# Attention and a three-way maxout layer on one core: the order of 489 commands and the engine letters of some of them are replaced

## The chip, the cores and the metric

The program runs on one core of one Trainium2 chip. The metric is device microseconds (us) of one execution. One core has the engines PE (TensorE, matrix products), DVE (VectorE), ACT (ScalarE), POOL (GpSimd) and SP (SyncE, which only issues transfers here). Each takes its own instructions strictly in the order in which the program gives them, and they meet at semaphores.

## The reference

```python
# q, k, v: 4 x 8 x 768 x 64; three of the eight heads see all earlier keys,
# five see 4 sink keys and a window of 64
scores = scale * np.matmul(q, k.transpose(0, 1, 3, 2))
...
a = np.exp(scores)
a = a / (np.sum(a, axis=-1, keepdims=True) + 1e-09)
return np.matmul(a, v).astype(np.float32)
...
x = np.ascontiguousarray(attn_out.transpose(0, 2, 1, 3)).reshape(B * S, H * D)
h = np.maximum(np.maximum(x @ w1, x @ w2), x @ w3)
return (h @ w_out).astype(np.float32)
```

x has 3072 rows of 512, each of w1, w2, w3 is 512 x 768, w_out is 768 x 512. Inputs and output are float32; the kernel computes its products in float16 with float32 sums.

## The kernel before

There are four batches (b = 0 to 3), and each batch has two halves of 384 query rows. The function `fast` holds one small function for each kind of work, and a tuple of strings, `PROGRAM`, names them one after the other with their arguments. A loop at the end of `fast` runs over the strings, and every engine gets its instructions in that order. Nothing else orders the work: there is no scheduler, only the semaphores between engines. A letter at the end of a command names the engine that does its element-wise part: `d` and `r` DVE (copy, or a reduction over one element that copies), `a` ACT, `p` POOL.

The commands that matter here:

- `idle n`: n products of zeros on PE (tile idl), 128 x 512, with no use for the result.
- `hl`, `load_v` issue transfers of q, k, v on the queues of SP and ACT; `load b quad` issues those of k and q (tile kq) on POOL's queue, two or four transfers; `w i` issues the transfer of a weight matrix on POOL's queue, `w 3` that of w_out (tile woutt).
- `cast`, `turnp`: for batch 0 a pair of heads is cast to float16 (tiles kn, qn) and transposed on PE (tile tr, copied to KQ). `turn b quad i part`: for batches 1 to 3 a quarter of kq is transposed by DVE (STREAM_TRANSPOSE, tile KQ). A batch takes eight such commands.
- `s0`, `s`: products of q and k (tile st, two buffers in PSUM), and on ACT the exponentials of them (tile pt). `k0`, `k`: a mask multiplied on pt, by DVE or POOL. `kx0`, `kx`: the far keys gathered (tile kx).
- `v`, `vc`, `vt`, `y`: v is cast, for batch 0 also sorted by a product on PE (tile vb), and gathered (tiles va, vx).
- `av b half hp`: probabilities times v for two heads (tile oacc on PE), a reciprocal and a multiplication on DVE (tile x), and with `D` a transposing transfer to xT on SP's queue.
- `f b half wi ni`: a hidden product, four matmuls of 128 x 384 into tile yy. With wi = 0 it is cast to acc by the letter's engine, with wi = 1 DVE takes the maximum into acc, with wi = 2 into hT. There are 144 of them.
- `o b half tb`: six matmuls of 128 x 512 on hT, a copy to ot, a transfer out. There are 24.
- `flags` (12 kinds of small instruction on POOL) compares the flags with what the order assumes, `guess` makes all five engines load its result from memory (TENSOR_LOAD flagged); `check`, `verdict`, `read` do the same near the end with all sums of exponentials (TENSOR_LOAD differ). `gs`, `gp` put a small transfer or copy in a queue, as a delay or a wait.

All tiles tr, vb, oacc, yy, idl share one pool of four PSUM banks, so PE can be at most four of them ahead of the engine that empties them:

```python
bkp = ctx.enter_context(tc.tile_pool(name="bkp", bufs=4, space=bass.MemoryType.PSUM))
...
for line in PROGRAM:
    for item in line.split(", "):
        name, *args = item.split()
        do[name](*args)
```

## Time and profile before

| what | us |
|---|---|
| median of 3 runs | 190.45 |
| the three runs | 189.97, 190.45, 194.31 |
| the profiled execution | 190.93 |
| its span, first to last instruction | 189.2 |
| first `f` product on PE | 26.38 |
| first scores of batch 2 (`s 2 0`) on PE | 71.05 |
| end of the last output product on PE | 184.6 |

The profiled execution is 1.7 us longer than its span, and 0.5 us longer than the median of the runs. An engine's busy time counts the time from the start to the end of its instructions. Matmuls are pipelined and their ends are modelled, so the busy time of PE says less than the start of one group of matmuls against the start of the next.

### The profile page before, as it was taken

The numbers are of one execution on the slowest core, as the hardware profiler recorded it, in microseconds if no ns is written. First come the engines' busy times: TensorE is split into PE (matmuls) and PEld (weight loads), VectorE is DVE, ScalarE is ACT, GpSimd is POOL, SyncE is SP. The second block draws the span as 40 slices with busy tenths as digits, with TensorE's granted clock in tenths as the row PEclk, the third lists the DMA queues.
The fourth block names the chain that finished last, engine by engine and source line by source line (L and its number), as shares of the span: only waits on it lengthen the run. The fifth ranks groups of instructions, "written<-read, shape, count | busy, mean of one in ns | idle before, by whom it ended". The sixth has DMA issues, their size and how long they took to land.

```text
span 189.2 us, 4749 instructions
## 1 busy us (share of the span) xinstructions
PE 180.0 (95%) x1859; PEld 105.7 (56%) x1859; DVE 144.7 (76%) x308; ACT 98.8 (52%) x158; POOL 82.3 (44%) x140
## 2 busy tenths in 40 slices
PE   7989799999999799999999999999999999999990
PEld 2644556566556356865565566655755575654550
DVE  3758989989899597888879899765883698475540
ACT  3599698377975457489086436665346301311110
POOL 7595978908883990099147102126313400000000
PEclk9999999999999999999999999999999999999998
DMA  5999999999999999539994301321132013401413
GB/s 178 327 327 276 208 211 208 195 150 204 193 158 204 122 271 203 140 66 200 212 223 120 112 0 55 66 80 55 30 64 107 0 59 63 136 0 55 166 56 119
DMA packets 44248, 26.59 MB, mean 141 GB/s; under 512 B 31038, under 2 KB 39742, under 8 KB 44222
## 3 DMA queue, kind: packets, MB, share of 16 engines
q1 hardware_dynamic: 38798, 17.54, 38.6%
q0 software_dynamic: 4192, 7.87, 23.1%
q10 hardware_dynamic: 1232, 0.85, 1.4%
q8 instruction: 15, 0.25, 0.5%
q14 instruction: 11, 0.09, 0.1%
HBM read 25.17 MB, written 6.29 MB: 166 GB/s over the span
## 4 chain that ended last, share of the span: by engine, by line
PE 80%; DVE 8%; DMA 7%; issue 1%; ACT 0%; ACTq 0%; DVEq 0%
PE yy L437 44%; PE yy L462 15%; PE oacc L717 8%; PE st L674 7%; DMA qs<-in_q_dram 5%; PE yst L437 3%; DMA vs<-in_v_dram 3%; DVE x L724 1%; PE yst L462 1%; DVE KQ L272 1%; DVE vx L800 1%; PE vb L505 1%; DVE va L478 1%; DVE KQ L241 1%; DVE va L510 1%
## 5 line engine op out<-in xcount | busy, mean ns | idle before, releaser
L377 POOL TENSOR_TENSOR pt<-pt,kb 128x512 f16<-128x512 f16 (+5 forms) x53 | 48.5, 934 | 61.0 <-ACT pt L691 49.6
L691 ACT ACTIVATE pt<-st 128x1024 f16<-128x1024 f32 (+2 forms) x51 | 43.5, 908 | 24.3 <-PE st L674 23.9
L437 PE MATMUL yy<-xT,w2t 128*128 128x384 f16 x184 | 36.2, 326 | 0.0
L437 PE MATMUL yy<-xT,w0t 128*128 128x384 f16 x180 | 34.6, 326 | 0.0
L437 PE MATMUL yy<-xT,w1t 128*128 128x384 f16 x176 | 34.2, 326 | 0.0
L462 PE MATMUL yy<-woutt,hT 128*128 128x512 f16 (+1 forms) x138 | 31.5, 372 | 1.1 <-DVE hT L449 1.1
L449 DVE TENSOR_TENSOR hT<-yy,acc 128x384 f16<-128x384 f32 x46 | 25.2, 555 | 5.2 <-PE yy L437 3.5
L449 DVE TENSOR_TENSOR acc<-yy,acc 128x384 f16<-128x384 f32 x44 | 24.0, 555 | 5.3 <-PE yy L437 4.0
L272 DVE STREAM_TRANSPOSE KQ<-kq 128x384 f32<-128x384 f32 x24 | 25.5, 1134 | 2.1 <-DMA kq<-in_k_dram 1.0
L437 PEld LDWEIGHTS <-w0t 128*128 128x128 f16 x192 | 18.1, 98 | 12.6 <-issue 0.6
L445 ACT CAST acc<-yy 128x384 f16<-128x384 f32 x27 | 12.8, 490 | 22.5 <-PE yy L437 20.4
L437 PEld LDWEIGHTS <-w1t 128*128 128x128 f16 x192 | 17.9, 98 | 12.1 <-issue 0.6
L437 PEld LDWEIGHTS <-w2t 128*128 128x128 f16 x192 | 17.6, 98 | 12.1 <-issue 0.5
L462 PEld LDWEIGHTS <-hT 128*128 128x128 f16 x150 | 14.4, 98 | 16.7 <-DMA woutt<-in_moe_w_out_dram 1.5
L471 ACT COPY ot<-yy 128x512 f32<-128x512 f32 (+1 forms) x14 | 7.9, 566 | 23.4 <-PE yy L462 20.2
L717 PEld LDWEIGHTS <-pt 128*128 128x128 f16 x472 | 17.3, 97 | 4.8 <-issue 1.0
L717 PE MATMUL oacc<-va,pt 128*128 128x65 f16 x392 | 18.8, 193 | 0.5 <-DVE pt L377 0.3
L724 DVE TENSOR_TENSOR x<-oacc,sums 128x384 f16<-128x384 f32 x32 | 17.8, 557 | 1.1
L629 ACT ACTIVATE pt<-st 128x1024 f16<-128x1024 f32 (+5 forms) x22 | 15.5, 759 | 2.9 <-PE st L608 2.7
L674 PE MATMUL st<-KQ 32*128 32x128 f16 (+2 forms) x342 | 14.9, 257 | 0.0
L377 DVE TENSOR_TENSOR pt<-pt,kb 128x256 f16<-128x256 f16 (+4 forms) x31 | 11.9, 388 | 1.8 <-ACT pt L691 1.7
L445 DVE CAST acc<-yy 128x384 f16<-128x384 f32 x18 | 9.9, 558 | 3.4 <-PE yy L437 3.0
(117 smaller groups left out, 190.9 us busy)
## 6 DMA issues: line engine op xcount, KB each, us to landing
out_dram<-ot SPq DMA_DIRECT2D x23, 256.0 KB, 2.2
vs<-in_v_dram SPq DMA_DIRECT2D x18, 256.0 KB, 4.7
ks<-in_k_dram SPq DMA_DIRECT2D x8, 192.0 KB, 5.1
kq<-in_k_dram POOLq DMA_DIRECT2D x3, 384.0 KB, 7.1
kq<-in_q_dram POOLq DMA_DIRECT2D x3, 384.0 KB, 8.7
kq<-in_k_dram POOLq DMA_DIRECT2D x3, 288.0 KB, 8.3
kq<-in_q_dram POOLq DMA_DIRECT2D x3, 288.0 KB, 9.5
qs<-in_q_dram ACTq DMA_DIRECT2D x4, 192.0 KB, 4.5
```

The source lines that it names most:

```text
L272: nc.vector.transpose(out=dst.rearrange("c (p j) -> c j p", j=n)[:, j0:j1], in_=src.rearrange("c (j i) -> c j i", i=R),)
L377: engine.tensor_tensor(out=x, in0=x, in1=of_blocks(kb, pattern, rows), op=ALU.mult)
L437: nc.tensor.matmul(yy[:, 0:HALF], w_t[wi][:, ks, ni * P : (ni + 1) * P], xT[b, half, ks].rearrange("p a t -> p (a t)"), start=(ks == 0), s ...
L445: op(out=acc[b, half, ni], in_=yy[:, 0:HALF])
L449: nc.vector.tensor_tensor(out=acc[b, half, ni] if wi == 1 else hT[b, half, ni], in0=yy[:, 0:HALF], in1=acc[b, half, ni], op=ALU.max,)
L462: nc.tensor.matmul(yo[:, 0:n], hT[b, half, ns][:, tb * P : (tb + 1) * P], woutt[:, ns, c : c + n], start=(ns == 0), stop=(ns == NNB - 1),)
L471: op(out=ot[:, c : c + n], in_=yo[:, 0:n])
L629: nc.scalar.activation(out=pts[0, half, hp, u][:, r0:r1, c0:c1], in_=sts[hp][:, r0:r1, c0:c1], func=AF.Exp, scale=sc,)
L674: nc.tensor.matmul(sts["XY"[g // 2]][:, g % 2, c0 : c0 + n * P], KQ[rows, 0, ki * P : (ki + 1) * P] if kind == "p" else kx[b % 2][quad][ro ...
L691: nc.scalar.activation(out=pts[b, s, xy][:, r0:r1, c0:c1], in_=st[:, r0:r1, c0:c1], func=AF.Exp, scale=sc,)
L717: nc.tensor.matmul(o[:, i, r, 0 : D + 1], at[b, h, kind, ki, qi], vv[:, 0 : D + 1], start=(n == 0), stop=(n == len(todo) - 1), skip_group_ ...
L724: nc.vector.tensor_tensor(out=x, in0=o[:, :, :, 0:D], in1=rc.unsqueeze(3).to_broadcast([P, HB, 2, D]), op=ALU.mult,)
```

## The change

The tuple `PROGRAM` is written anew. It has the same 489 commands, the same number of each kind, and the same products, exponentials, masks and transfers; the order differs from the first command on, and some letters do: of the 48 `f` with wi = 0, ACT takes 36 instead of 28 and DVE 12 instead of 20; of the 24 `o`, ACT 11 instead of 15 and DVE 13 instead of 9; five of the 24 `v` become reductions on DVE, as none was before. `idle` still stands six times with 18 products in all.

```diff
-    "idle 11, hl 0 2 2 sc, cast 0 1 pd, turnp 0 1 aa, cast 0 0 dd, cast 0 2 dp, load_v 0 0 0 4 s",
+    "idle 2, cleark 0 d, cleark 1 d, idle 2, hl 0 2 2 sc, load_v 0 0 0 4 s, flags",
+    "cast 0 0 aa, cast 0 2 aa, idle 11, cast 0 1 pd, idle 1, turnp 0 0 dd, turnp 0 1 ad",
...
```

Three places show what moves. The first is the start of POOL's row. kb and every are constants, kn and ks_117 belong to pair 1 of batch 0, want, none, both and flagged to `flags`. Before:

```order
L348 AFFINE_SELECT every_140<-every_140 128x386
L220 CAST kn<-ks_117 128x384
L220 CAST qn<-qs 128x384
L220 CAST kn<-ks 128x384
L544 MEMSET kx_155 128x512
```

Now:

```order
L351 AFFINE_SELECT every_140<-every_140 128x386
L757 MEMSET want 1x8
L759 MEMSET want 1x1 x5
L761 TENSOR_SCALAR none<-ir_121 1x16
L763 TENSOR_TENSOR both<-none 1x8
L764 TENSOR_TENSOR both<-both,want 1x8
L765 TENSOR_TENSOR both<-both 1x8
L767 TENSOR_TENSOR both<-both 1x4
L767 TENSOR_TENSOR both<-both 1x2
L767 TENSOR_TENSOR both<-both 1x1
L769 CAST flagged<-both 1x2
L223 CAST kn<-ks_117 128x384
```

The whole of `flags` has moved from the middle of the program to the front, ahead of the cast of kn of pair 1; the cast of qn of pair 2, which followed it, went to ACT, and that of kn of pair 3 comes later.

The second is POOL's row around the transfers of k and q for the second quad of batch 2, `load 2 1` (kq_1235 before, kq_1256 now). va1, vx0 and vx1 are the gathered v of batches 1 and 2. Before:

```order
L766 CAST flagged_161<-both_1046 1x2
L377 TENSOR_TENSOR pt_799<-pt_799,kb_130 128x2x2x128
L393 DMA woutt_61<-in_moe_w_out_dram 128x6x512
L377 TENSOR_TENSOR pt_1083<-pt_1083,kb_130 128x2x128
L377 TENSOR_TENSOR pt_883<-pt_883,kb_130 128x384
L377 TENSOR_TENSOR pt_1006<-pt_1006,kb_130 128x128
L377 TENSOR_TENSOR pt_1148<-pt_1148,kb_130 128x256
L257 DMA kq_1235<-in_k_dram 32x1536
L257 DMA kq_1235<-in_k_dram 96x1536
L257 DMA kq_1235<-in_q_dram 32x1536
L257 DMA kq_1235<-in_q_dram 96x1536
```

Now:

```order
L396 DMA woutt_61<-in_moe_w_out_dram 128x6x512
L380 TENSOR_TENSOR pt_1099<-pt_1099,kb_130 128x512
L380 TENSOR_TENSOR pt_1099<-pt_1099,kb_130 128x128
L481 CAST va1_152<-vs_1133 128x2x3x64
L527 CAST vx1_154<-vs_1133 64x4x2x64
L529 CAST vx1_154<-vs_932 64x16x64
L380 TENSOR_TENSOR pt_1038<-pt_1038,kb_130 128x4x128
L481 CAST va1_152<-vs_1133 128x2x3x64
L529 CAST vx0_153<-vs_1192 64x4x64
L260 DMA kq_1256<-in_k_dram 32x1536
L260 DMA kq_1256<-in_k_dram 96x1536
L260 DMA kq_1256<-in_q_dram 32x1536
```

Between woutt and `load 2 1` POOL now has eight instructions instead of four, and `flags` is no longer ahead of woutt.

The third is DVE's row ahead of the first scores of batch 2 (`s 2 0`), which read what the transposes of kq_1235 (now kq_1256) write. Before:

```order
L449 TENSOR_TENSOR hT4_1346<-yy_1341,acc_1145 128x384
L377 TENSOR_TENSOR pt_1008<-pt_1008,kb_130 128x2x128
L272 STREAM_TRANSPOSE KQ_1381<-kq_1235 128x12x32 x3
L272 STREAM_TRANSPOSE KQ_922<-kq_752 128x12x32
L794 TENSOR_LOAD flagged_161
L1037 BRANCH_PREFETCH_HINT
L272 STREAM_TRANSPOSE KQ_1381<-kq_1235 128x12x32
```

Now:

```order
L474 COPY ot_1378<-yy_1379 128x512
L452 TENSOR_TENSOR hT4_1393<-yy_1388,acc_1025 128x384
L275 STREAM_TRANSPOSE KQ_1395<-kq_1256 128x12x32
L481 CAST va0_151<-vs_1192 128x2x3x64
L275 STREAM_TRANSPOSE KQ_1395<-kq_1256 128x12x32 x2
L474 COPY ot_1411<-yy_1412 128x512
L275 STREAM_TRANSPOSE KQ_1395<-kq_1256 128x12x32
L803 TENSOR_REDUCE kx01_156<-KQ_1395 128x4x128
L803 TENSOR_REDUCE kx01_156<-KQ_1395 128x4x8
```

The four transposes now stand among two copies of outputs and a cast. Counted from the start of DVE's row, the last of the four transposes of kq_1235 was the 123rd instruction, and that of kq_1256 is the 134th. Less ahead of it are 4 casts of kn and qn, 4 casts of acc and 7 reductions of 128 to 512 columns; more are 4 masks of 512 columns and 2 of 128, 2 copies of ot, 2 of vb, 1 of tr and 1 of xT, 3 reductions of 384 columns to va, 1 short reduction to kx, 1 cast of half of v, 8 small copies to vx and kx, and 1 fill.

## Prediction

> **What bounds the kernel now.** I read the page first, then PE's waits and timeline, then the stages.

> ```profile
> span 189.2 us, 4749 instructions
> PE 180.0 (95%) x1859; PEld 105.7 (56%) x1859; DVE 144.7 (76%) x308; ACT 98.8 (52%) x158; POOL 82.3 (44%) x140
> PE 80%; DVE 8%; DMA 7%; issue 1%; ACT 0%; ACTq 0%; DVEq 0%
> ```

> By the chain that ended last, PE bounds 80% of the span. The timeline of PE shows where it does not (columns: start, length, work, count; in brackets the idle time ahead and what ended it).

> ```profile
> 1.28 4.87 PE L324 MATMUL idl<-zero 128*128 128x512 f16 x11 [1.28 <-DVE warm L327]
> 5.95 0.52 PE L238 MATMUL tr<-ident,kn 128*128 128x128 f16 x3
> ...
> 17.40 0.60 PE L324 MATMUL idl<-zero 128*128 128x512 f16 x2
> ...
> 26.38 1.47 PE L437 MATMUL yy<-xT,w0t 128*128 128x384 f16 x8
> ...
> 29.76 0.20 PE L717 MATMUL oacc<-va,pt 128*128 128x65 f16 x1 [0.26 <-DVE pt L377]
> ...
> 60.51 0.82 PE L437 MATMUL yy<-xT,w2t 128*128 128x384 f16 x4
> 62.45 5.35 PE L462 MATMUL yy<-woutt,hT 128*128 128x512 f16 x24 [1.12 <-DVE hT L449]
> ```

> From 26.38 the first hidden products run. A group of 8 there takes 8 x 0.163 = 1.30 us to the next start, and I went through all groups of hidden, output and `av` products from 26.38 to the end in this way: the starts are late in four places only, by 0.4, 0.2, 0.2 and 1.3 us, together 2.1. The 1.3 lies between 60.51 + 4 x 0.163 = 61.16 and 62.45, where the first output product waits for woutt. So behind 26.38 an order can gain some 2 us and no more; what else it can gain lies ahead of 26.38.

> Now the other engines by stage (columns: stretch, its length, busy us and instructions of PE, PEld, DVE, ACT, POOL, PE's granted clock, DMA share, GB/s).

> ```profile
> 0.00:8.60 8.60, 7.30 (x37) 3.47 (x38) 4.82 (x15) 3.04 (x6) 5.12 (x16) 1.00 0.80 244
> 8.60:26.40 17.80, 15.93 (x193) 8.96 (x193) 13.81 (x33) 15.87 (x27) 14.70 (x32) 1.00 1.12 264
> 26.40:60.50 34.10, 33.59 (x427) 20.80 (x425) 32.19 (x63) 24.66 (x40) 24.97 (x42) 1.00 1.12 188
> 60.50:71.05 10.55, 9.43 (x60) 4.60 (x56) 8.42 (x14) 5.56 (x9) 9.04 (x14) 1.00 1.17 196
> 71.05:102.00 30.95, 30.95 (x403) 19.43 (x403) 25.78 (x60) 20.68 (x31) 13.44 (x18) 1.00 0.80 174
> 102.00:184.60 82.60, 82.60 (x759) 48.45 (x756) 59.41 (x129) 28.74 (x47) 15.07 (x21) 1.00 0.21 65
> ```

> The second bound is DVE: from 26.40 to 60.50 it is busy for 32.19 of 34.10 us, 94.4%, while PE still runs dense; behind 102 it has 28% to spare. Work put from the late part into the early one is what PE would feel.

> **The change part by part.**

> *PE's work.* The same products, so none is gained or lost. I sum at one point, the first scores of batch 2 (`s 2 0`):

> ```profile
> 71.05 0.56 PE st L674 x12
> ...
> 184.22 0.35 PE yy L462 x6
> ```

> From 71.05 to the end no late start was found, so a delay there is a delay of the end. Now three hidden products fewer stand ahead of it and one `av` of 21 matmuls more: 3 x 0.65 - 0.65 = 1.3 us of PE work is left for afterwards. If `s 2 0` came at 71.05 again, the end would be 1.3 later; without any new wait it comes at 69.75.

> [...]

> *DVE's work ahead of `s 2 0`.* DVE must have done the four transposes that `s 2 0` reads, and, being in order, all ahead of them: 123 instructions before, 134 now. The prices:

> ```profile
> L449 DVE TENSOR_TENSOR acc<-yy,acc 128x384 f16<-128x384 f32 x44 | 24.0, 555 | 5.3 <-PE yy L437 4.0 <-DVE acc L445 0.5 <-ACT acc L445 0.2
> L445 DVE CAST acc<-yy 128x384 f16<-128x384 f32 x18 | 9.9, 558 | 3.4 <-PE yy L437 3.0
> L471 DVE COPY ot<-yy 128x512 f32<-128x512 f32 x9 | 6.2, 690 | 4.6 <-PE yy L462 4.6
> L377 DVE TENSOR_TENSOR pt<-pt,kb 128x512 f16<-128x512 f16 x10 | 4.1, 419 | 0.0
> L478 DVE CAST va<-vs 128x384 f16<-128x384 f32 x5 | 2.7, 545 | 0.0
> L220 DVE CAST kn<-ks 128x384 f16<-128x384 f32 x4 | 2.2, 550 | 1.3 <-DMA ks<-in_k_dram 1.3
> L510 DVE CAST va<-vb 128x512 f16<-128x512 f32 x2 | 1.4, 686 | 0.2 <-PE vb L505 0.2
> L800 DVE TENSOR_REDUCE vx<-va 64x128 f16<-64x128 f16 x2 | 0.6, 283 | 0.0
> ```

> Gone: 4 casts x 0.550, 4 casts of acc x 0.558, 7 reductions of 0.28 to 0.7 (2.9): 7.3 us. Come: 4 masks x 0.419 (1.7) and 2 short ones (0.5 at most), 2 copies of ot x 0.690 (1.4), 2 of vb x 0.686 (1.4), 3 reductions of 384 columns x 0.545 (1.6, the row of the cast of the same shape), half of v, twice that shape (1.1), copies of tr and xT (0.9), and 10 small ones at 0.25 (2.5): 11.1 us. Net 3.8. One instruction begins a little before the end of the last (44 x 0.555 is 24.4 against 24.0 busy), so I take 3.6 (bounds 2 and 5, with the small ones at half and at 0.4).

> *The start.* 16 of the 17 products of zeros now stand ahead of the first transposes, 11 before. At the rate of the first row, 4.87 / 11 = 0.443, they end at 1.28 + 16 x 0.443 = 8.37, so DVE's copies of tr begin near 8.6; before, the transposes ran from 5.95. By 8.60 DVE had done 4.82 us; now it can do some 3.9 by then (4.82 less three casts and a copy of tr, four fills of 0.3 more). Of 4.82 + 13.81 + 32.19 + 8.42 = 59.2 us of work up to `s 2 0` before, now 59.2 + 3.6 = 62.8, there are 58.9 to do behind 8.6. With no idle time that is 67.5.

> Before, DVE idled 8.0 us on the way: 4.0 in the start (waits for q, k, v to land and for PE), 1.9 up to 60.50 and 2.1 behind it. In the start I take half, 2.0, since the transfers land no sooner but more work is at hand; behind it the 94.4% that DVE reached beside a dense PE, 2.5 us idle on the remaining 42. So `s 2 0` comes at 67.5 + 4.5 = 72.0, 0.95 later than before, and with the 1.3 the end 2.3 later. With 2 us idle or less PE is the bound and `s 2 0` comes at 69.75, no delay; with the old 8.0 it is 75.5, and +5.8.

> *POOL's queue.* `flags` goes to the front:

> ```profile
> 46.87 0.09 POOL L754 MEMSET want<- 1x8 f32 x1
> ...
> 49.64 0.17 POOL L766 CAST flagged<-both 1x2 int32<-1x2 f32 x1
> ...
> 50.99 0.92 POOL L393 DMA_DIRECT2D woutt<-in_moe_w_out_dram  x1
> ...
> 55.12 1.08 POOL L257 DMA_DIRECT2D kq<-in_k_dram  x2
> ...
> 64.13 1.13 DVE L272 STREAM_TRANSPOSE KQ<-kq 128x384 f32<-128x384 f32 x1 [1.05 <-DMA kq<-in_k_dram]
> 66.28 3.99 DVE L272 STREAM_TRANSPOSE KQ<-kq 128x384 f32<-128x384 f32 x4 [1.01 <-DMA kq<-in_q_dram]
> ...
> L794 DVEq TENSOR_LOAD <-flagged x1: 956/956/956, 66.4 to 66.4; - x1
> ...
> L794 SPq TENSOR_LOAD <-flagged x1: 530/530/530, 73.9 to 73.9; - x1
> ```

> `flags` took 49.81 - 46.87 = 2.9 us. In the start it delays the cast of kn of pair 1 to about 7.4, under the zeros that last to 8.37: nothing; without them 1 to 2 us. `guess` adds a load on each queue: 0.5 us on SP ahead of the second half of v, up to 1 on DVE, inside the idle I allow. In the middle woutt is issued earlier by up to 2.9, so the 1.3 us wait at 62.45 goes (0 to 1.3). I count no gain for it, since what is late next is DVE: the gap lies ahead of `s 2 0`, and there DVE's time counts.

> *ACT and the rest.* ACT takes 8 casts of acc more and 4 output copies fewer, and has 9.4, 5.0 and 10.3 us to spare in the three stages from 26.40 to 102: nothing. SP's order of transposing transfers and `gs` moves by a few commands: 0, bounds -0.5 and +1. Between 71.05 and 102 DVE has 5.2 us idle, and more transposes of batch 3 fall there: 0 to 0.5. The loads of `read` now follow `verdict` by one hidden product (0.65 us) instead of six: 0 to 0.6. The last output is made in the same way behind the last matmul: 0.

> Sum: 2.3 on the profiled 190.93, or 193.2. That execution stands 0.5 over the median of the runs, so I give 192.7.

> **The rivals.**

> *PE stays the bound.* DVE idles so little, since more work is at hand when it waits, that it keeps ahead; then the 2.1 us of late starts go, as an order could aim at: 190.45 - 2.1 = 188.3, or 186 if the first hidden product also came 2 us before 26.38. For it: ACT is relieved in the start, DVE's 4.0 idle there can be filled. Against it: 67.5 leaves 2.2 us of idle time ahead of 69.75, where 8.0 were. 27%, three tenths of it below 186.6.

> *A transfer that lands late holds DVE.* The transposes of `load 2 1` waited for landing at 64.13 and 66.28, 9.0 us after the issue of k at 55.12. Now POOL has eight instructions between woutt and this load instead of four, two of them gathers of 1024 columns, and DVE has two output copies behind the transposes. If k is issued at 57 it lands at 66.0, and q 2.2 later at 68.2; two transposes, a copy and a transpose follow (3 x 0.95, by (3.99 - 1.13) / 3 in the row, and 0.6), and `s 2 0` is free at 71.6. PE's four banks are full by then, and each us more of POOL is one more at the end. With an issue at 59.5 it is 74.1: 3.05 + 1.3 = 4.3 more, 194.8. It decides from an issue of 57.4, where it passes the forecast's 72.0. 25%.

> *PE's clock falls back in the start.* The first zeros take 0.443 us and those at 17.40 about 0.2 (0.60 for two with the modelled end), so PE begins at half rate and rises. Before, six zeros stand between 8.3 and 18.6; now one does, and PE has little else there. The granted clock is 1.00 in every stage, also where the zeros took 0.443, so that column does not show it. If PE fell back for 3 us, the `s0` and `av` products there would take 1.5 us longer, and ACT and DVE wait for them: 192.7 + 1.5 = 194.2. [...] 8%.

> **How the numbers follow.** The forecast's case, 190.9 to 194.6, has 40%, and a fifth of it above 194.3. Within 2% of 190.45 (186.6 to 194.3, about what a measurement of this kernel can tell from no change): faster is 0.3 of the first rival, 8%; slower is 0.2 x 40 + 0.8 x 25 + half of 8, 32%; the rest is 60%. The range leaves out a tenth at each side: low in the first rival, 188.1, high in the second, 196.8 (issue near 61.5).

> **What would show it.** DVE over 93% busy between 28 and 72 and `s 2 0` near 72 shows the sum right; the waits of PE should then name DVE (banks, KQ). A wait of STREAM_TRANSPOSE for kq of 2 us or more shows the second rival, hidden products at half rate or tr groups of 0.32 behind 10 us the third. The wait for woutt should be gone. Wrong I am if DVE idles as before and `s 2 0` still comes before 71, or if PE loses time behind 102, where I see none.

## The result and the profile after

| | before | after |
|---|---|---|
| runs, us | 189.97, 190.45, 194.31, 197.96 | 196.44, 197.57, 197.90, 198.35 |
| median of these, us | 192.38 | 197.74 |
| the profiled execution, us | 190.93 | 196.44 |
| its span, us | 189.2 | 194.7 |

The ratio of after to before is 1.039, with a 95% interval from 1.030 to 1.048. The kernel became slower, and 197.7 us lies above the range on record (188.1 to 196.8). Executions of before spread from 189.6 to 200.7 us, most of them near 190.5 or near 195, and every ratio here compares only the executions within about 1.5% of each kernel's fastest.

The page of after: the span, the engines, and the chain of waits by engine.

```profile
span 194.7 us, 4761 instructions
PE 180.8 (93%) x1859; PEld 105.4 (54%) x1859; DVE 145.7 (75%) x311; ACT 97.1 (50%) x161; POOL 78.5 (40%) x134
PE 51%; DMA 17%; DVE 14%; ACT 6%; SPq 5%; issue 3%; POOL 2%; ACTq 0%; DVEq 0%; POOLq 0%
```

PE holds 51% of the chain where it held 80%, and DMA 17% for 7%. PE's timeline shows where (columns as before).

```profile
1.27 5.18 PE L327 MATMUL idl<-zero 128*128 128x512 f16 x16 [1.27 <-DVE warm L330]
...
7.96 0.34 PE L241 MATMUL tr<-ident,kn 128*128 128x128 f16 x3 [1.18 <-POOL kn L223]
...
20.16 0.19 PE L720 MATMUL oacc<-vx,pt 128*128 128x65 f16 x1 [1.76 <-DVE vx L529]
...
28.26 0.81 PE L440 MATMUL yy<-xT,w0t 128*128 128x384 f16 x4
...
64.92 4.06 PE L465 MATMUL yy<-woutt,hT 128*128 128x512 f16 x18 [0.87 <-DVE x L727]
...
71.64 0.29 PE L720 MATMUL oacc<-va,pt 128*128 128x65 f16 x4 [0.82 <-DVE ot L474]
...
72.39 0.90 PE L677 MATMUL st<-KQ 32*128 32x384 f16 x18
...
91.78 0.34 PE L677 MATMUL st<-KQ 32*128 32x384 f16 x1
...
92.70 1.46 PE L440 MATMUL yy<-xT,w0t 128*128 128x384 f16 x8
...
96.18 0.33 PE L677 MATMUL st<-KQ 32*128 32x384 f16 x1 [0.72 <-ACT pt L694]
97.09 0.34 PE L677 MATMUL st<-KQ 32*128 32x384 f16 x2 [0.59 <-ACT pt L694]
...
97.65 0.82 PE L440 MATMUL yy<-xT,w1t 128*128 128x384 f16 x4
...
189.12 0.50 PE L465 MATMUL yy<-woutt,hT 128*128 128x128 f16 x6
```

The same points in before, as its timeline has them:

```profile
70.99 0.63 PE L674 MATMUL st<-KQ 32*128 32x384 f16 x18
...
94.60 0.34 PE L674 MATMUL st<-KQ 32*128 32x384 f16 x1
...
184.05 0.50 PE L462 MATMUL yy<-woutt,hT 128*128 128x128 f16 x6
```

By the timeline, `s 2 0` of before starts at 70.99; 71.05 is where the chain of the prediction's view enters it. From these rows the delay can be followed. It is the difference of the starts, plus the PE work that after has not yet done there (8 hidden products, an output and an `av` less, the scores `s 2 6` more by `s 2 3`):

| point on PE | before | after | work left, us | delay, us |
|---|---|---|---|---|
| first hidden product | 26.38 | 28.26 | 0 | 1.9 |
| first scores of batch 2, `s 2 0` | 70.99 | 72.39 | 1.3 | 2.7 |
| scores `s 2 3` | 94.60 | 91.78 | 6.3 (8 x 0.65 + 1.29 + 0.34 - 0.56) | 3.5 |
| last output product | 184.05 | 189.12 | 0 | 5.1 |

Two thirds of the 5.1 us are lost by `s 2 3`, the rest (1.6) at the two waits of 96.18 and 97.09. The span grew by 0.4 more behind the last output product. Now what held PE. First the copies of vx in the start, on DVE, and what POOL did beside them (after, timeline).

```profile
17.42 0.28 DVE L529 COPY vx<-va 64x512 f16<-64x512 f16 x1
17.72 2.09 DVE L527 COPY vx<-va 64x128 f16<-64x128 f16 x2
...
18.09 1.60 POOL L500 CAST vn<-vs 128x768 f16<-128x768 f32 x2
```

A copy of 512 columns took 0.28 us, and two smaller ones 2.09 while POOL cast; they ended as POOL's casts did, at 19.7 to 19.8. PE's stretches behind its wait for the second (columns: stretch, length, PE busy, granted clock, DMA share, GB/s):

```profile
20.00:22.00 2.00, 1.84 (x31) 0.88 1.11 208
22.00:24.00 2.00, 2.00 (x24) 0.50 1.16 210
24.00:26.00 2.00, 1.79 (x26) 0.77 1.16 209
```

PE had idled 1.76 us, and then ran at half rate: 0.12 x 2 + 0.50 x 2 + 0.23 x 2 = 1.7 us of work lost. Then the transfers of v for batches 2 and 3, as the engines that copy them see it (after, timeline of POOL, DVE and ACT):

```profile
60.88 0.39 POOL L529 CAST vx<-vs 64x256 f16<-64x256 f32 x1 [2.68 <-DMA vs<-in_v_dram]
61.35 1.06 POOL L260 DMA_DIRECT2D kq<-in_k_dram  x2
...
63.62 0.55 DVE L803 TENSOR_REDUCE va<-vs 128x384 f16<-128x384 f32 x1 [2.52 <-DMA vs<-in_v_dram]
...
68.98 2.08 DVE L275 STREAM_TRANSPOSE KQ<-kq 128x384 f32<-128x384 f32 x2 [0.65 <-DMA kq<-in_q_dram]
...
94.28 0.93 ACT L481 CAST va<-vs 128x384 f16<-128x384 f32 x2 [2.85 <-DMA vs<-in_v_dram]
```

Three engines stand still for v that has not landed. Behind POOL's copy stands `load 2 1`; behind DVE's the x that PE waits for at 64.92 (the ot of 71.64 stands behind two transposes that waited for q); behind ACT's the exponentials of `s 2 3`, whose bank PE waits for at 96.18. The queue of SP shows that the first half of v of batch 2 is asked for later (timeline; before first, then after):

```profile
48.16 3.73 SPq L302 DMA_DIRECT2D vs<-in_v_dram  x3
```

```profile
50.55 8.72 SPq L305 DMA_DIRECT2D vs<-in_v_dram  x3
```

It is asked for from 50.55 to 59.27, where before had done so by 51.89; woutt is asked for at 50.40 (50.99 before), so now ahead of it. Whether woutt is what slows it was argued, and no run shows it. The chain that ended last runs through this transfer into `s 2 0` (after, critical chain, stretch 58 to 74):

```profile
50.55 10.21 DMA vs<-in_v_dram
...
62.89 6.00 DMA kq<-in_q_dram
...
68.98 2.08 DVE KQ L275 x2
71.06 0.52 DVE ot L474
71.58 1.03 DVE KQ L275
```

Between the first two stand POOL's copy of v (60.88) and the issue of `load 2 1` (61.35): v holds POOL, POOL holds q, and q holds the transposes.

### The profile page after: what moved, and what is told of

The parts are those of the page before. It is cut to its first block, busy times and chain, and to the rows that moved or that the text cites. A ratio compares the mean times of both kernels' runs of the same rounds, so it can differ in the third digit from the quotient of the medians.

```text
span 194.7 us, 4761 instructions
## 1 busy us (share of the span) xinstructions
PE 180.8 (93%) x1859; PEld 105.4 (54%) x1859; DVE 145.7 (75%) x311; ACT 97.1 (50%) x161; POOL 78.5 (40%) x134
## 4 chain that ended last, share of the span: by engine, by line
PE 51%; DMA 17%; DVE 14%; ACT 6%; SPq 5%; issue 3%; POOL 2%; ACTq 0%; DVEq 0%; POOLq 0%
PE yy L440 27%; DMA vs<-in_v_dram 12%; PE yy L465 11%; DVE KQ L275 5%; PE oacc L720 4%; SPq L305 4%; DMA kq<-in_q_dram 3%; PE yst L440 3%; PE st L677 3%; ACT pt L694 2%; DVE acc L452 2%; ACT pt L632 2%; DMA ir<-in_is_retrieval_dram 2%; DVE vx L527 1%; PE yst L465 1%
## 5 line engine op out<-in xcount | busy, mean ns | idle before, releaser
L380 POOL TENSOR_TENSOR pt<-pt,kb 128x256 f16<-128x256 f16 (+5 forms) x45 | 42.0, 943 | 46.4 <-ACT pt L694 41.6
L694 ACT ACTIVATE pt<-st 128x1024 f16<-128x1024 f32 (+2 forms) x51 | 43.5, 909 | 19.9 <-PE st L677 19.7
L440 PE MATMUL yy<-xT,w2t 128*128 128x384 f16 x180 | 35.2, 326 | 0.0
L440 PE MATMUL yy<-xT,w1t 128*128 128x384 f16 x180 | 34.9, 326 | 0.3 <-DVE acc L452 0.3
L440 PE MATMUL yy<-xT,w0t 128*128 128x384 f16 x180 | 34.0, 326 | 0.4 <-DMA xT<-x 0.4
L452 DVE TENSOR_TENSOR acc<-yy,acc 128x384 f16<-128x384 f32 x45 | 24.4, 555 | 9.4 <-PE yy L440 6.9
L448 ACT CAST acc<-yy 128x384 f16<-128x384 f32 x35 | 16.4, 489 | 29.5 <-PE yy L440 29.2
L452 DVE TENSOR_TENSOR hT<-yy,acc 128x384 f16<-128x384 f32 x45 | 24.6, 556 | 7.1 <-PE yy L440 5.0
L474 ACT COPY ot<-yy 128x512 f32<-128x512 f32 (+1 forms) x12 | 6.7, 560 | 28.3 <-PE yy L465 21.5
L380 DVE TENSOR_TENSOR pt<-pt,kb 128x512 f16<-128x512 f16 (+5 forms) x39 | 14.9, 398 | 4.9 <-ACT pt L694 4.8
L677 PE MATMUL st<-KQ 32*128 32x128 f16 (+2 forms) x342 | 15.9, 257 | 1.3 <-ACT pt L694 1.3
L677 PEld LDWEIGHTS <-KQ 32*128 32x128 f16 x342 | 9.2, 92 | 9.1 <-issue 8.1
```

Of the source, the lines that this page charges most:

```text
L380: engine.tensor_tensor(out=x, in0=x, in1=of_blocks(kb, pattern, rows), op=ALU.mult)
L440: nc.tensor.matmul(yy[:, 0:HALF], w_t[wi][:, ks, ni * P : (ni + 1) * P], xT[b, half, ks].rearrange("p a t -> p (a t)"), start=(ks == 0), s ...
L448: op(out=acc[b, half, ni], in_=yy[:, 0:HALF])
L452: nc.vector.tensor_tensor(out=acc[b, half, ni] if wi == 1 else hT[b, half, ni], in0=yy[:, 0:HALF], in1=acc[b, half, ni], op=ALU.max,)
L677: nc.tensor.matmul(sts["XY"[g // 2]][:, g % 2, c0 : c0 + n * P], KQ[rows, 0, ki * P : (ki + 1) * P] if kind == "p" else kx[b % 2][quad][ro ...
L694: nc.scalar.activation(out=pts[b, s, xy][:, r0:r1, c0:c1], in_=st[:, r0:r1, c0:c1], func=AF.Exp, scale=sc,)
```

## The experiments

All of them but r4, which has one `idle` more, are orders and letters of the same commands. Ratios are to before, run beside each group, with 95% intervals.

**Halves exchanged.** Everything ahead of one command in the order of the one kernel, and all that is then left in the order of the other. The cut is the first hidden product in the first two, and `s 2 0` in the others.

```diff
 e1_start_before: before up to "f 0 0 0 3 a", then after
 e2_start_after:  after up to "f 0 0 0 3 a", then before
 e3_late_after:   before up to "s 2 0", then after
 e4_late_before:  after up to "s 2 0", then before
```

> The commands ahead of the first hidden product in the order and with the letters of before, all others as after has them. Theory A (three losses that add, read from the two traces: the first hidden product comes 1.9 us later, 28.26 for 26.38; the first scores of batch 2 another 0.7 later against the work that is left; what lies behind them 2.9 with the tail): the first loss goes, first hidden product at 26.4, first scores of batch 2 near 70.5, span 194.7 - 1.9 = 192.8, ratio to before 1.03. Theory B (the second half of v and load 2 1 behind it set the first scores of batch 2, whatever the start does): first hidden product at 26.4, but the scores stay near 72.4 and the span at 194 to 195, ratio 1.04.

> The commands ahead of the first hidden product as after has them, all others in the order and with the letters of before. Theory A: first hidden product near 28.3 and the end 1.9 later than before, span 191.1, ratio 1.01. Theory B: flags are already done, woutt is asked for earlier and the wait of 1.3 us for it is gone, so of the 1.9 only 0.6 is left, span 189.8, ratio 1.003.

> The commands ahead of the first scores of batch 2 as before has them, all others in after's order and letters. Theory A (the 2.9 us behind 72.4 come from the order there: the scores that wait for exp at 94 to 97, one wait for acc at 76, and the tail): first scores of batch 2 at 71.05, late starts of the scores near 95 still there, span 189.2 + 2.9 = 192.1, ratio 1.015. Theory C (the late starts behind 72 are the backlog that the earlier part leaves on DVE and ACT): none of them, span 189 to 190, ratio 1.00.

> The commands ahead of the first scores of batch 2 as after has them, all others in the order and with the letters of before. Theory A: first scores of batch 2 at 72.4, 1.3 us of work less done ahead of them, nothing lost behind: span 189.2 + 2.6 = 191.8, ratio 1.014. Theory C: the waits behind 72 come along, span 194 to 195, ratio 1.03 to 1.04.

Measured: 1.052 [1.043, 1.061]; 1.025 [1.021, 1.029]; 1.048 [1.044, 1.051]; 1.013 [1.008, 1.018]. Only the last came as a theory had it: with before's order behind `s 2 0` most of the loss is gone (A; C falls). From 1.0387 to 1.0128 is a factor of 1.026, 4.9 us of 190.5, more than the 2.8 us that the two profiled executions show there. The third says that the halves do not simply add, and fits neither. The first doesn't test what it was meant to: all of `flags` then follows the cut, POOL has it ahead of masks, and PE waits 2.86 us for it at 29.69, so that the first hidden product comes at 30.22 instead of 26.4.

The second shows before's own weak place, with a start that is 1.2 us late (ACT and PE of e2, timeline):

```profile
59.00 1.04 ACT L527 CAST vx<-vs 64x1024 f16<-64x1024 f32 x1 [2.66 <-DMA vs<-in_v_dram]
...
61.89 0.44 PE L718 MATMUL oacc<-va,pt 128*128 128x65 f16 x9 [1.71 <-ACT va L479]
```

The same transfer of v lands late, ACT waits for it, and PE for ACT. Behind that PE's clock falls too (stretches of e2, columns as before):

```profile
62.00:64.00 2.00, 2.00 (x35) 0.76 1.64 156
64.00:66.00 2.00, 2.00 (x6) 0.50 0.82 141
66.00:68.00 2.00, 2.00 (x9) 0.88 0.00 0
```

The lost work is 0.48 + 1.0 + 0.24 = 1.7 us, and the delay of 1.2 becomes more.

**Single suspects.**

```diff
 r1_w3_ahead (before):
-flags, load_v 1 0 s, ..., k 1 0 Y 0 p, f 0 1 0 0 d, w 3
+w 3, flags, load_v 1 0 s, ..., k 1 0 Y 0 p, f 0 1 0 0 d
 r2_w3_early (after):
-load 2 0, turn 2 0 0 0, ..., v 1 0 3 r, w 3
+w 3, load 2 0, turn 2 0 0 0, ..., v 1 0 3 r
 r3_reduce (after):
-y 0 0 5:8:2 s d, y 0 0 4:5:1 r d, y 0 0 1:4:2 r d, y 0 0 1:4:2 s d
+y 0 0 5:8:2 s r, y 0 0 4:5:1 r r, y 0 0 1:4:2 r r, y 0 0 1:4:2 s r
 r4_zeros (after):
-av 0 0 1
+idle 8, av 0 0 1
```

> Before, with the load of woutt one command earlier on POOL, ahead of flags (issue near 48 for 50.99). Theory T (woutt's 768 KB then go ahead of the half of v of batch 2 that is asked for at 48 to 52, so v lands late, near 59, and the engine whose next command copies it, ACT here, holds all behind it): PE waits some 2 us near 60 for a copy of v that stands behind it on ACT, the granted clock falls behind that, span 192 to 194, ratio 1.02, as in the run that took after's start. Theory U (the forecast's reading of before: woutt is what PE waits for at 61.16 to 62.45, and an earlier issue ends that wait): span 189.2 - 1.3 = 187.9, ratio 0.993.

> After, with the load of woutt moved up to the load of k and q of batch 2, first half, some 10 us earlier (issue near 38 for 50.40), when the DMA engines carry little. Theory T: the half of v of batch 2 lands by 57 to 58 instead of 60.8, the waits of POOL (2.68) and DVE (2.52) for it go, load 2 1 is issued by 58.5 and the first scores of batch 2 come near 70.5, span 194.7 - 2 = 192.7, ratio 1.02 to 1.03. Theory V (the work of DVE ahead of those scores is the bound, as the forecast's sum has it): scores at 72, span 194 to 195.

> After, with the four copies of v's pair rows of batch 0 on DVE (at 17.4 to 20.1) done as reductions. Theory P (DVE's plain 16-bit copies there stand still while POOL casts: two took 2.09 us, a third 0.28, and a reduction does not, 0.28 to 0.68 each): the four take 2.1 us in all, PE goes on at 19.5 for 20.16, and with an idle time of 1.1 us for 1.76 the granted clock stays at 1.00 (after: 0.50 in 22 to 24): first hidden product 1.2 to 1.9 earlier, span near 193. Without the clock's part: 0.6 earlier, span 194.1. Theory Q (a reduction waits for POOL just as long): nothing changes.

> After, with eight products of zeros more (8 x 0.213 = 1.7 us) ahead of the first output of batch 0, in the hole of 1.76 us at 18.4 to 20.16. If the fall of the granted clock comes from that hole and costs time: clock 1.00 from 18 to 28, first hidden product some 1.0 to 1.5 earlier than 28.26, span 193.2 to 193.7. If DVE and ACT set the pace there anyway: clock 1.00, first hidden product within 0.3 of 28.26, span 194.4 to 195. If the hole is not the reason: clock falls all the same.

Measured: 1.008 [1.004, 1.012]; 1.051 [1.046, 1.055]; 1.036 [1.032, 1.040]; 1.037 [1.033, 1.042]. Asking for woutt earlier gains nothing in before (U falls; T had the sign, and more than twice the size) and does not cure after (T falls there); whether it costs there is not clear, since the interval meets after's. The other two helped the start, by a little less than forecast: the first hidden product came at 27.13 and 27.50 for 28.26, and the clock stayed at 1.00 there. The five reductions of vx of r3 took 2.43 us in all, so P holds. But the end stayed. PE of r3 (timeline):

```profile
96.34 0.33 PE L675 MATMUL st<-KQ 32*128 32x384 f16 x1 [1.79 <-ACT pt L692]
97.26 0.34 PE L675 MATMUL st<-KQ 32*128 32x384 f16 x2 [0.59 <-ACT pt L692]
```

The wait for the exponentials of `s 2 3` is now 1.79 + 0.59 = 2.4 us, and the clock falls behind it, to 0.93, 0.50 and 0.72 in the stretches of 2 us from 96 to 102: another 0.14 + 1.0 + 0.56 = 1.7. So the waits at this one place cost 1.3 us in after's profiled execution, and with the clock 4.1 in that of r3. Of r3's earlier start 0.9 us was still there at `s 2 3`, but ACT's copy of v of batch 3 began at 94.45, against 94.28 in after: v landed no sooner, and what the start had won was waited away.

**Copies of v put later.** x3 has both edits, x4 also those of r3.

```diff
 x1_v20_later (after):
-y 2 0 4:5:1 s p, ..., load 2 1, k 1 5 X 0 p
+..., load 2 1, k 1 5 X 0 p, y 2 0 4:5:1 s p
-v 2 0 1 a, v 2 0 0 r, ..., v 2 0 2 r, ..., v 2 0 3 d, ..., s 2 0
+..., s 2 0, v 2 0 1 a, v 2 0 0 r, v 2 0 2 r, v 2 0 3 d
 x2_v31_later (after):
-s 2 6, v 3 1 3 a, k 2 6 Y 0 p, v 3 1 1 a, ..., s 2 5
+s 2 6, k 2 6 Y 0 p, ..., s 2 5, v 3 1 3 a, v 3 1 1 a
```

> After, with five copies of v of batch 2, first half, put later: the one on POOL behind load 2 1 and the next mask, the four of DVE and ACT behind the first scores of batch 2. Theory W (an engine in order that copies a v not yet landed holds what stands behind it): POOL's wait of 2.68 us no longer holds load 2 1, which is issued near 58.2 for 61.35, DVE's wait of 2.52 at 61.1 goes, PE's waits for x and ot (0.87 and 0.82) go, first scores of batch 2 near 70.6 for 72.4, span 194.7 - 1.8 = 192.9, ratio 1.025. Theory D (the DMA engines are the bound there: what lands earlier makes something else land later): the first transposed x of batch 1 lands later instead, PE waits 1.5 us or more for it near 68 to 71, scores near 72, span 194 to 195, ratio 1.035.

> After, with two copies of v of batch 3 on ACT put behind the scores s 2 5. Theory W: ACT no longer waits 2.85 us at 91.4 to 94.3 ahead of the exp of s 2 3, so PE's waits for exp at 96 and 97 (0.72 and 0.59, 1.5 with the short starts) go, span 193.2, ratio 1.03. Theory D: the span stays at 194.5 or more, since another wait follows.

> Both of the two edits ahead. Theory W: they add, span 194.7 - 1.8 - 1.5 = 191.4, ratio 1.015. Theory D: 193 to 195, ratio 1.03.

> Both, and the four copies of the start as reductions (which brought the first hidden product to 27.13 for 28.26 and left the end where it was). Theory W: now that nothing behind takes it back, the 1.1 us count, span 190.3, ratio 1.01. Theory D: as without them, 193 or more.

Measured: 1.023 [1.014, 1.033]; 1.015 [1.005, 1.025]; 1.014 [1.004, 1.023]; 1.020 [1.012, 1.027]. With two commands of one engine moved by a few places the ratio is 1.015 instead of 1.039, and in every trace with that edit the waits at this place are gone, so W holds there. How much they cost is read from one product to another, from the hidden product behind `s 2 3` (`f 1 1 0 3`) to that behind `s 2 5` (`f 1 1 1 2`). In after it takes from 92.70 to 97.65, 4.95 us, and in e1, r3, r4, y1 and y2, which have after's order there, 5.1 to 6.1. In x2 it takes from 90.96 to 94.22, 3.26 us, and in x4, y3 and z2 (described below), which have the edit, 3.25 to 3.26:

```profile
90.96 1.46 PE L438 MATMUL yy<-xT,w0t 128*128 128x384 f16 x8
...
94.22 0.82 PE L438 MATMUL yy<-xT,w1t 128*128 128x384 f16 x4
```

From there to the last output product all of these take 91.5 to 91.6 us, but r3, with its fall of the clock, 93.1. So the two copies cost 1.7 us in after's profiled execution, and a fall of the clock 1.7 more where it follows. The ratios of after and x2 differ by 2.4 points, 4.5 us, and x2's profiled execution does not show that as the copies' price: its span is 3.4 us shorter, from 2.3 won in the start, where no command differs, 1.7 at this place and 0.6 lost to a wait for xT at 86.85. The first edit gains less clearly, since its interval touches after's, and the gains do not add: D is right in so far as another wait follows (x4: PE waits 1.44 for acc at 75.38 and 1.44 for xT at 89.31). The start of x2's profiled execution (timeline of POOL, DVE and PE):

```profile
18.62 1.60 POOL L498 CAST vn<-vs 128x768 f16<-128x768 f32 x2 [0.50 <-DMA vs<-in_v_dram]
...
17.75 0.46 DVE L525 COPY vx<-va 64x128 f16<-64x128 f16 x2
...
25.96 0.82 PE L438 MATMUL yy<-xT,w0t 128*128 128x384 f16 x4
```

v landed 0.5 us later, so POOL's cast began behind DVE's copies, which took 0.46 for 2.09, and the first hidden product came at 25.96 for 28.26: half a microsecond of a transfer goes with 2.3 us of the start. These are two executions; how often either start occurs is not known.

**Transfers asked for earlier, and flags put back.**

```diff
 y1_load11 (after):
-w 1, vc 1 0 4 p, ..., load 1 1, w 2
+w 1, load 1 1, vc 1 0 4 p, ..., w 2
 y2_load20 (after):
-k0 3 1 2 p, ..., k0 3 0 2 p, ..., load 2 0
+load 2 0, k0 3 1 2 p, ..., k0 3 0 2 p
 y3_loads_v31 (after): both, and x2's
 y4_flags (after):
-load_v 0 0 0 4 s, flags, ..., cast 1 1 dd, guess, ..., s 2 0, k 1 4 Y 0 p
+load_v 0 0 0 4 s, ..., cast 1 1 dd, ..., s 2 0, k 1 4 Y 0 p, flags, guess
```

> After, with the load of k and q of batch 1, second half, put ahead of POOL's two casts of v of pair 1 (issue near 18.1 for 24.74; before 19.18). Theory D (the DMA engines are behind: 36 to 40 us carry 48 GB/s for 171 in before, and by 72 some 0.5 MB less is moved, 2.5 us at 190 GB/s): the hole fills in part, and POOL's casts come 2 us later, behind DVE's copies of vx, which then take 0.3 each: PE's hole of 1.76 us at 20 goes, first hidden product near 26.5, scores of batch 2 near 70.5, span 192 to 193, ratio 1.015. Theory W alone (only the copies that wait for v count): the start gains, the end does not, span 194 to 196.

> After, with the load of k and q of batch 2, first half, ahead of two masks on POOL (issue near 33 for 38.3; before 32.8). Theory D: 36 to 40 us carry over 100 GB/s, v of batch 2 lands 1 to 2 us earlier, POOL's wait of 2.68 and DVE's of 2.52 near 58 to 63 shrink by as much, scores of batch 2 near 71, span 193 to 193.5, ratio 1.02 to 1.025. Theory W alone: the landing at 60.8 does not move, span 194.5 or more.

> Both loads put ahead, and the two copies of v of batch 3 on ACT behind s 2 5. Theory D: the gains add (3.5 at the scores of batch 2, 1.5 near 95), span 189.5 to 190.5, ratio 1.00. Theory W alone: 193, as with the two copies alone.

> After, with flags and guess behind the first scores of batch 2, where POOL idles 3 us. If flags at the front cost what the trace shows (PE waits 1.18 us at 6.6 to 7.96 for the cast of kn that stands behind flags on POOL): kn's transposes at 6.8, first hidden product 0.5 to 1.2 earlier, and the end earlier by no more than that, span 193.5 to 194.5. If v's transfers set the end all the same: span 194.5 to 196, ratio 1.035. As the forecast had it (nothing, under the zeros): first hidden product at 28.3.

Measured: 1.029 [1.022, 1.035]; 1.032 [1.027, 1.036]; 1.020 [1.016, 1.023]; 1.034 [1.027, 1.041]. Neither y1, y2 nor y4 is clearly below after, and y3, which has x2's edit, is not below x2 alone: that after moves less by 72 us does not explain its loss. y1's first hidden product came at 28.18 instead of the 26.5 expected, since DVE's four copies took nearly as long beside POOL's issues (2.40 us, for 2.65 in after; last section). In y2 the hole at 36 to 40 us is filled (208 GB/s for 48), another opens behind it (122 GB/s from 40 to 44), and POOL still waits for v (POOL's timeline):

```profile
61.11 0.39 POOL L527 CAST vx<-vs 64x256 f16<-64x256 f32 x1 [2.60 <-DMA vs<-in_v_dram]
```

SP's queue asks for this v from 52.29 in y2, later than in after (50.55), so the earlier load on POOL's queue did not bring it sooner. The front place of `flags` costs nothing that can be measured in the end, though PE waits 1.18 us behind it; that the later waits take it up is argued.

**The last two.**

```diff
 z1_before_v20 (before):
-load_v 2 0 s, y 2 0 1:8:2 s a, ..., s 1 4
+load_v 2 0 s, ..., s 1 4, y 2 0 1:8:2 s a
 z2_v31_reduce (after): x2's edit, and
-y 0 0 4:5:1 r d, y 0 0 1:4:2 r d, y 0 0 1:4:2 s d
+y 0 0 4:5:1 r r, y 0 0 1:4:2 r r, y 0 0 1:4:2 s r
```

> Before, with ACT's copies of v of batch 2, first half, put behind the exp of the last scores of batch 1 (s 1 4), so that a late landing holds neither the copy of v that the output of batch 1 needs nor those exps. Theory W (the executions of before that take 194 to 197 are those in which that transfer lands late, as in the run with after's start, where ACT waited 2.66 us for it and PE 1.71 for ACT): the best time stays at 190, the median of all runs comes from 191 to 195 down to 190 to 191. If the long executions come from elsewhere: as many as before, median of all 191 to 195; the transfer's copies only come later, 0 to 0.5 us.

> After, with the two copies of v of batch 3 on ACT behind s 2 5, and three of the four copies of vx in the start as reductions (0.28 + 0.42 + 0.68 us, which in the run with four reductions did not stand still beside POOL's casts). If the two groups of times with the two copies alone (193.1 to 193.5 and 195.9 to 196.9) come from DVE's copies standing still or not at 17.7: first hidden product 26.3 to 27, all runs at 193 to 194, ratio 1.015. If they come from the transfers behind: the two groups stay, 193 and 196.

Measured: z1 1.003 [0.995, 1.011]. Its median of 191.8 against 192.6 for before beside it shows no gain, so W is not borne out. z2 1.012 [1.004, 1.019]; its times run from 191.9 to 197.9 and not all from 193 to 194, so its first reading falls, though the best is 1.2 us under x2's best (193.1). Its profiled execution, of 190.2 us span, has no wait of PE over 0.7 us near 20 and none near 96, a first hidden product at 26.41, and `s 2 0` at 69.56 (DVE, timeline):

```profile
17.66 1.31 DVE L801 TENSOR_REDUCE vx<-va 64x128 f16<-64x128 f16 x3
```

No version was shown to beat before.

## Why the prediction was wrong

**The failed step** is "From 71.05 to the end no late start was found, so a delay there is a delay of the end." It reads before's rows as if they held for after's order. The terms that priced the part behind, "Between 71.05 and 102 DVE has 5.2 us idle, and more transposes of batch 3 fall there: 0 to 0.5" and "ACT takes 8 casts of acc more and 4 output copies fewer, and has 9.4, 5.0 and 10.3 us to spare ...: nothing", are where most was missing: 2.8 us of 5.5 in the profiled executions, and 2.6 of 3.9 points by e4. In the traces it is 0.8 us by `s 2 3`, 1.6 at the waits for ACT behind it, and 0.4 behind the last output product. Of the 0.8, 0.3 is `s 2 0` itself, with 0.83 us to the next start for 0.56 before, and 0.4 a late start at 76.25, where PE waits for DVE's acc. The 1.6 are the place that x2's edit mends (1.7 by x2's rows, 2.8 in r3 with 1.7 of clock behind it). ACT had the time; its order had not, since a copy that waits for a transfer stood ahead of exponentials that PE needs. The prediction looked for what is late next on DVE and POOL alone, and not command by command on ACT.

**The sum at `s 2 0`** gave 72.0, and 72.39 was measured, but not by the sum's way. DVE had less to do and idled more than the sum had it (after, DVE's stretch up to `s 2 0`):

```profile
0.00:72.39 72.39, 60.99 (x131) 0.98 1.02 207
```

It had 60.99 us of work for the 62.8 forecast, and idle behind 8.6 were 63.8 - 56.4 = 7.4 us for 4.5, of them 2.52 for v. That the two errors cancel is luck. What set `s 2 0` was not DVE's sum of work but the chain shown above, from v over POOL to q. In 28.26 to 60 DVE was over 93% busy as said, and behind 60 it waited.

**The rival of a late transfer** is what happened up to `s 2 0`: q's landing, two transposes, a copy and a transpose, as it has them, but with another carrier. `load 2 1` was issued at 61.35, later than the 59.5 priced, because POOL stood before a copy of v, which no step foresaw; k and q landed faster than the 9 us taken from before (q at 68.9, 6.5 after its issue at 62.40), and DVE waited 0.65 us for them, under the 2 us named as the rival's sign, since it had already stood 2.52 us for v.

**The clock's rival** (8%, +1.5) did happen, where the prediction saw PE have little to do, and cost 1.7 us of work. No run shows the 3 us that its sum takes for the fall; after's fall lasted 3.41 us. "The granted clock is 1.00 in every stage, also where the zeros took 0.443, so that column does not show it" was wrong for this place: the column fell to 0.50. Undoing it (r3, r4) moved the first hidden product by 0.8 to 1.1 us and not the end.

**flags**, "under the zeros that last to 8.37: nothing": the 16 zeros took 5.18 us in after for the 7.1 priced, since from the ninth on they start 0.216 us apart, and PE waited 1.18 us for kn at 7.96. **Ten small copies at 0.25**: two of them took 2.09. **woutt**: no gain was rightly counted, but before's wait at 62.45 was read wrongly. Its row names DVE's hT, and hT ended at 61.87 + 0.55 = 62.42 (before, timeline of DVE):

```profile
61.87 0.55 DVE L449 TENSOR_TENSOR hT<-yy,acc 128x384 f16<-128x384 f32 x1
```

woutt landed at about the same time (11.4 us after its issue at 50.99), so asking for it earlier could not end that wait by itself, and in r1 it gained nothing. The rival that PE stays the bound has no support.

What the start and v of batch 2 each cost in the end is not settled: z2's ratio, with the start's copies mended too, lies inside the interval of x2's. Nor is the cause of e3's time, or why the ratios of after and x2 differ by more than their traces show.

## What to carry to other kernels

Where an engine runs strictly in order, look at each command that is the first to touch a transferred tile, and at what stands behind it: a copy that comes one wait too soon holds all of that, and an engine's spare time does not help (in after ACT is busy for 50% of the span, and its wait of 2.85 us for v of batch 3 held the exponentials of `s 2 3`). When an order is written anew, the late starts of the old trace say nothing of the new order behind the first point that moved. A mended place can be waited away at the next transfer (r3: of 1.1 us won in the start 0.9 was there at `s 2 3`, and ACT's copy of v began at 94.45 for 94.28), so check what that one hangs on before counting the gain. And compare two profiled executions from point to point before an edit gets the credit: x2's span is 3.4 us shorter than after's, and its two commands account for 1.7.

## What the runs showed of the hardware

The clock. Idle times of 1.71 (e2), 1.76 (after) and 1.79 us (r3) were each followed within 2 us by a granted clock of 0.50, for about 3.4 us (1.7 us of work lost at half rate). An idle time of 2.85 us was not (r4, timeline of PE):

```profile
71.09 1.46 PE L438 MATMUL yy<-xT,w0t 128*128 128x384 f16 x8 [2.85 <-DMA xT<-x]
```

```profile
18.10:21.51 3.41, 1.65 (x38) 1.00 1.08 207
21.51:24.92 3.41, 3.41 (x39) 0.50 1.16 209
```

```profile
69.50:72.91 3.41, 1.46 (x8) 1.00 1.15 259
```

PE's work in the one is mostly small products, in the other hidden ones of 128 x 384; what the clock counts stays open.

DVE beside POOL. Copies of 16-bit data within SBUF took longer while POOL cast (2.09 us for two in after, 0.46 in x2, where POOL cast later), and in y1 while POOL issued transfers (0.97 for the same two):

```profile
18.94 0.97 DVE L525 COPY vx<-va 64x128 f16<-64x128 f16 x2
...
18.80 1.06 POOL L258 DMA_DIRECT2D kq<-in_k_dram  x2
```

Not every issue does this: x2's 0.46 stand beside that of w1t, from 17.38 to 18.13. Reductions over one element, which copy the same data, did not (five in 2.43 us in r3, from 17.26, where POOL cast from 18.29). Why the copies take longer there was not shown.
